# Induced attention followed by an ELU feed-forward: the opening and the ramp of the first batch in another written order

## The chip, the cores and the metric

One core of a Trainium2 chip runs the whole program. The metric is the device time of one execution in microseconds; the time before is the median of three runs. An execution has five engines with a list of instructions each: TensorE (PE, matmuls and transposes), VectorE (DVE), ScalarE (ACT), GpSimd (POOL) and SyncE (SP, which here only issues transfers). Each works its list in order and waits for the others by semaphores.

## What is computed

```python
scale = 1.0 / np.sqrt(C)                       # C = 128
def mab(q, kv):
    s = scale * (q @ kv.transpose(0, 2, 1))
    s = s - s.max(-1, keepdims=True)
    a = np.exp(s)
    a /= a.sum(-1, keepdims=True) + 1e-09
    return a @ kv
h = mab(I, x)                                  # I: 32 inducing points; x: 4 x 12480 x 128
y = mab(x, h).reshape(49920, 128)
f = y @ w_in                                   # w_in: 128 x 2048
g = np.where(f > 0.0, f, np.exp(np.minimum(f, 0.0)) - 1.0)
return g @ w_out                               # w_out: 2048 x 128
```

The weights come as float64, so the kernel sees each as pairs of 32-bit words.

## The kernel before, in words

A batch of 12480 rows is cut into 25 blocks of 480 or 512 rows, grouped in seven groups g = 0 to 6. The first attention of a batch gives h (32 x 128). It needs x transposed (xT), the scores of the inducing points, their running bounds in three phases for the first batch (`bias_of`), exponentials, and a gather of x with them. h times w_in gives the weight `hw` of 128 rows: three copies of 32 rows in high and low parts, and a row block of ones. The second attention of a block gives a stack `stk` (L576), and one matmul of `hw` with it is attention and first feed-forward layer at once (`ffn_in`, L613).

The long part is a loop over units. A unit is a block and a pair of chunks (256 of 2048 columns) of the feed-forward layer; a block has eight, planned as PPNPDPDP. For each, TensorE fills `ph`, ScalarE takes the exponential (e, L627), VectorE joins both branches (L633), then the result is split in a high part gh (ScalarE, L642) and a low part gl (GpSimd L655 for P, VectorE L649 for D, none for N), and TensorE adds up `po` from gh and gl with the second weight's high and low parts wo_h and wo_l, or from e with wo_n (`ffn_out`, L682). The output matmuls of unit n stand three to five units behind its input matmul in TensorE's list. `sum_excess` (L657) sums the second weight once, ahead of unit 7's output matmuls.

Only the first batch is not hidden. Its steps stand in `FIRST` (L35), a list of names that is worked from left to right; what a step issues is appended to its engines' lists in that order (TensorE, VectorE and ScalarE keep it; GpSimd and SyncE are put in order by the build in the unit loop). The names: x and y are the first and second half of a group's transposes with their copies to xT (`transpose_first`, L263, copies L290: VectorE for x, ScalarE for y), s and m the scores and their copy and maximum (L306), b the bound of a phase, w the exponentials (L378), e the transposed exponentials (L391), g and h the gather and its sum (L398). `sum`, `share`, `norm`, `spread`, `project`, `stack` make `hw` out of h, `room` allocates it and writes its ones (L483). l0 to l3 are the second attention of the first block alone (the lone block), a0 to a3 of the rest of group 0. u0, u1 and so on are the units: after a u the steps up to the next u are issued, in the loop of L856.

A to E, with a number s, turn part s of a weight into floating point: parts 0 to 3 are w_in, 4 to 7 are w_out, 512 columns each. A takes the exponent field out (VectorE L175, ScalarE L179), B makes a scale of it, bounded below and above (GpSimd L188 and L193; for some parts ScalarE L184 and L185 take the place of L188), C puts the mantissa together (VectorE L199, L203), D finishes (VectorE L209, product on GpSimd L213), E splits a part of w_out (ScalarE L236, L239, GpSimd L240) by chunks of 128. A part's exponent lies in one of two buffers of the pool `op`, so an A waits until the part two before it is done. The loads of the first batch stand in SyncE's list in the order of `first_batch` (L768): half of w_in, 14 pieces of x, the other half, four parts of w_out, which share buffers with later x.

Of the kernel before, what the change touches and what calls it, by code (L numbers as in the profile page):

```python
# [28 lines left out]


# [14 lines left out]
def kernel(  # L45
# [117 lines left out]
    class Weight:  # L163
# [17 lines left out]
        def scale_of(self, busy):  # L181
# [5 lines left out]
            else:  # L187
                nc.gpsimd.tensor_scalar(  # L188
                    out=self.scale, in0=self.part, scalar1=896.0, scalar2=1150.0,
                    op0=ALU.max, op1=ALU.min,  # L190
# [40 lines left out]
    def split_w_out(s, w):  # L231
        for i in range(WC):
            f = s * WC + i
            t = w.low[:, i * C : (i + 1) * C]
            if f in WHERE_N:
                nc.scalar.copy(wo_n[:, WHERE_N[f], :], t)  # L236
            if f in WHERE_S:
                n = WHERE_S[f]
                nc.scalar.copy(wo_h[:, n, :], t)  # L239
                nc.gpsimd.tensor_sub(wo_l[:, n, :], t, wo_h[:, n, :].bitcast(F32))  # L240
# [22 lines left out]
    def transpose_first(b, g):  # L263
# [9 lines left out]
        for v in range(0, U, UP):  # L273
# [13 lines left out]
            for i, half in enumerate(halves):  # L287
                m = min(2, nq - 2 * i)
                copy = nc.scalar.copy if v else nc.vector.tensor_copy
                copy(half[:, :, :, v : v + n], ps[:, 2 * i : 2 * i + m])  # L290
# [192 lines left out]
    def room_for_h(b):  # L483

        hw = hwp.tile([P, F], F32R, tag="hw", name=f"hw_{b}")
        nc.gpsimd.memset(hw[3 * Q :, :].bitcast(F32), 1.0)
# [430 lines left out]
```

## Time and profile before

| | us |
|---|---|
| median of three runs (1692.66 to 1695.55) | 1695.47 |
| the profiled execution | 1693.33 |
| its span in the trace | 1691.5 |
| TensorE busy | 1627.5 |
| ScalarE busy | 1478.7 |
| VectorE busy | 1428.5 |
| GpSimd busy | 1421.0 |

A row of the timeline reads: start and duration in us, engine, line of the kernel, operation, output and inputs with their shapes, and in brackets how long the engine was idle before it and what ended that. A row of the windows gives the busy time of TensorE, its weight loads, VectorE, ScalarE and GpSimd in a stretch, with the number of instructions, then the granted TensorE clock, the share of the DMA engines and GB/s. Rows that begin with a line number group all instructions of one kind: busy time and mean (page) or shortest, median and longest (view of a line).

### The profile page before, as it was taken

What the parts mean: (1) busy time and instruction counts of PE and PEld (TensorE: products, weight loads), DVE (VectorE), ACT (ScalarE), POOL (GpSimd) and SP (SyncE); (2) the same over time, 40 slices, a digit from 0 to 9 for tenths busy, and PEclk for the clock granted to TensorE, in tenths of its full rate; (3) what the DMA queues carried; (4) which work ended last, traced back from release to release, by engine and by line L of the source; (5) the groups of instructions that cost most, each with busy time, mean ns of one, the idle gap of its engine ahead of it and who ended that gap; (6) DMA issues with size and microseconds to landing.
All of it is one profiled execution on the core that took longest, in us unless ns stands there. A gap on an engine that the chain in (4) does not pass through costs nothing.

```text
span 1691.5 us, 23388 instructions
## 1 busy us (share of the span) xinstructions
PE 1627.5 (96%) x7656; PEld 1216.0 (72%) x7656; DVE 1428.5 (84%) x1479; ACT 1478.7 (87%) x1720; POOL 1421.0 (84%) x751
## 2 busy tenths in 40 slices
PE   6479999999999999999999999999999999999998
PEld 4246777777786777777877677777778777777886
DVE  6778888888889888888888888888888888888886
ACT  4368999999898999989989898899889999999996
POOL 4468888888898888888889898888888998998897
PEclk9689999999999999999999999999999999999999
DMA  7143324222314333232223423421322111110111
GB/s 252 40 83 67 62 49 82 53 50 73 75 38 79 52 75 69 45 73 58 57 66 55 78 48 63 82 50 22 79 44 44 28 25 35 34 37 16 33 28 24
DMA packets 384762, 98.18 MB, mean 58 GB/s; under 512 B 364864, under 2 KB 370784, under 8 KB 384384
## 3 DMA queue, kind: packets, MB, share of 16 engines
q1 hardware_dynamic: 384640, 96.68, 28.0%
q8 instruction: 61, 1.00, 0.3%
q14 instruction: 61, 0.50, 0.1%
HBM read 48.94 MB, written 25.56 MB: 44 GB/s over the span
## 4 chain that ended last, share of the span: by engine, by line
PE 72%; DVE 9%; ACT 7%; issue 6%; POOL 2%; DMA 2%; SPq 0%; POOLq 0%; DVEq 0%; ACTq 0%
PE po L704 51%; PE ph L619 17%; ACT e L627 4%; DVE e L633 3%; ACT gh L642 3%; POOL gl L655 1%; PE ps_t L532 1%; DVE xT L260 1%; DVE gl L649 1%; PE ps_s L313 1%; DVE ph L633 1%; PE ps_hh L404 1%; DMA xm<-in_x_dram 1%; DMA out_dram<-o 1%; DVE o L712 1%
## 5 line engine op out<-in xcount | busy, mean ns | idle before, releaser
L655 POOL TENSOR_TENSOR gl<-e,gh 128x1024 fp32r<-128x1024 f32 (+1 forms) x500 | 1169.5, 2355 | 213.2 <-ACT gh L642 201.6
L627 ACT ACTIVATE e<-ph 128x1024 f32<-128x1024 f32 (+1 forms) x800 | 800.8, 1002 | 122.8 <-PE ph L619 121.4
L633 DVE SCALAR_TENSOR_TENSOR e<-ph,e 128x1024 f32<-128x1024 f32 (+1 forms) x600 | 714.6, 1193 | 184.5 <-ACT e L627 178.6
L619 PE MATMUL ph<-stk,hw 128*128 128x512 f32 (+1 forms) x1600 | 541.3, 420 | 22.6 <-DVE e L633 15.9
L704 PE MATMUL po<-gh,wo_h 128*128 128x512 f32 (+1 forms) x1400 | 547.6, 391 | 11.1 <-ACT wo_h L239 6.8
L704 PE MATMUL po<-gh,wo_l 128*128 128x512 f32 (+1 forms) x1400 | 547.8, 391 | 2.6 <-POOL wo_l L240 2.6
L642 ACT ACTIVATE gh<-e 128x1024 fp32r<-128x1024 f32 (+1 forms) x500 | 518.6, 1037 | 27.5 <-DVE e L633 25.5
L704 PE MATMUL po<-gl,wo_h 128*128 128x512 f32 (+1 forms) x1400 | 433.0, 390 | 0.0
L619 PEld LDWEIGHTS ph<-stk,hw 128*128 128x128 f32 x1600 | 294.7, 190 | 170.8 <-issue 59.0
L704 PEld LDWEIGHTS po<-gh,wo_h 128*128 128x128 f32 x1400 | 263.6, 188 | 68.2 <-ACT wo_h L239 8.0
L704 PEld LDWEIGHTS po<-gl,wo_h 128*128 128x128 f32 x1400 | 264.2, 189 | 57.8
L704 PEld LDWEIGHTS po<-gh,wo_l 128*128 128x128 f32 x1400 | 263.8, 188 | 56.3 <-POOL wo_l L240 3.6
L633 DVE SCALAR_TENSOR_TENSOR ph<-ph,e 128x1024 f32<-128x1024 f32 (+1 forms) x200 | 239.5, 1198 | 30.2 <-ACT e L627 28.4
L649 DVE SCALAR_TENSOR_TENSOR gl<-ph,gh 128x1024 fp32r<-128x1024 f32 (+1 forms) x200 | 237.4, 1187 | 0.1
L642 ACT ACTIVATE gh<-ph 128x1024 fp32r<-128x1024 f32 (+1 forms) x200 | 201.1, 1005 | 4.3 <-DVE ph L633 3.9
L704 PE MATMUL po<-e,wo_n 128*128 128x512 f32 (+1 forms) x400 | 184.0, 582 | 0.0
L713 POOL TENSOR_TENSOR o<-o,excess 128x512 f32<-128x512 f32 (+1 forms) x100 | 126.6, 1266 | 4.4 <-DVE o L712 4.4
L704 PEld LDWEIGHTS po<-e,wo_n 128*128 128x128 f32 x400 | 75.4, 189 | 53.4 <-issue 46.0
L712 DVE STREAM_TRANSPOSE o<-po 128x512 f32<-128x512 f32 (+1 forms) x100 | 69.1, 691 | 4.9 <-PE po L704 4.9
L260 DVE STREAM_TRANSPOSE xT<-xq 128x1024 f32<-128x1024 f32 (+2 forms) x39 | 45.5, 1166 | 0.0
L592 POOL TENSOR_TENSOR alo<-aT,ahi 128x512 fp32r<-128x512 f32 (+3 forms) x27 | 34.2, 1269 | 0.8 <-ACT ahi L590 0.8
L404 PE MATMUL ps_hh<-xm,e 128*32 128x128 f32 (+2 forms) x872 | 31.1, 280 | 3.6 <-DVE h L421 2.0
(107 smaller groups left out, 552.6 us busy)
## 6 DMA issues: line engine op xcount, KB each, us to landing
xm<-in_x_dram SPq DMA_DIRECT2D x32, 512.0 KB, 4.8
out_dram<-o SPq DMA_DIRECT2D x240, 64.0 KB, 2.0
xq<-in_x_dram SPq DMA_DIRECT2D x84, 128.0 KB, 3.0
out_dram<-o SPq DMA_DIRECT2D x160, 60.0 KB, 1.9
stk<-ahi SPq DMA_DIRECT2D x118, 64.0 KB, 2.0
xq<-in_x_dram SPq DMA_DIRECT2D x60, 120.0 KB, 2.9
stk<-ahi SPq DMA_DIRECT2D x80, 60.0 KB, 2.0
stk<-alo SPq DMA_DIRECT2D x59, 64.0 KB, 2.0
```

The source lines that it names most:

```text
L260: nc.vector.transpose(t, xq.rearrange("p u d -> p (u d)"))
L404: nc.tensor.matmul(ps[c * Q : (c + 1) * Q, :C], st["e", g][:np_, u * Q : (u + 1) * Q], st["xm", g, u - u % UP][:np_, u % UP, :], start=(u ...
L592: eng.tensor_sub(alo, aT, ahi.bitcast(F32))
L619: nc.tensor.matmul(ph[:, i], state[b]["hw"][:, f * P : (f + 1) * P], stacks[b, k], start=True, stop=True,)
L627: nc.scalar.activation(e, ph, AF.Exp, bias=-1.0)
L633: nc.vector.scalar_tensor_tensor(out=v["g"], in0=v["ph"], scalar=1.0, in1=v["e"], op0=ALU.max, op1=ALU.min)
L642: nc.scalar.activation(v["gh"], v["g"], AF.Copy, bias=0.0 if how == "P" else -1.0)
L649: nc.vector.scalar_tensor_tensor(out=v["gl"], in0=v["g"], scalar=-1.0, in1=v["gh"].bitcast(F32), op0=ALU.add, op1=ALU.subtract,)
L655: nc.gpsimd.tensor_sub(v["gl"], v["e"], v["gh"].bitcast(F32))
L704: nc.tensor.matmul(po[:, :T], w, g, start=(cp == 0 and i == 0), stop=(cp == NCP - 1 and i == len(parts) - 1),)
L712: nc.vector.transpose(o.rearrange("p u d -> p (u d)"), po[:, :T])
L713: nc.gpsimd.tensor_tensor(out=o, in0=o, in1=excess.unsqueeze(1).broadcast_to([P, U, Q]), op=ALU.subtract)
```

## The change

The list `FIRST` is written anew. Group 1 opens instead of group 0, and all eight A stand ahead of the first unit, as do C, D of parts 4 and 5 and E of part 4. In detail:

- Of the 13 copies of transposed x that VectorE made, five stay (x of groups 1, 4 and 6), eight go to ScalarE (a table, `COPIES`).
- The first half of w_in is loaded behind four pieces of x, the second half ahead of the last piece (`LOADS`).
- ScalarE makes the bounds of parts 3 and 4 instead of 6 and 7.
- GpSimd's bounds are a min and then a max; they were a max and then a min.
- The ones of the first batch's `hw` come from ScalarE instead of GpSimd.
- E works on runs of neighbouring chunks, 512 or 256 columns, instead of 128. The split chunks are kept in their natural order, and `sum_excess` sums them in pieces of 256 columns.

```diff
-    x0 A0 A1 B0 x1 y0 C0 B1 D0 y1 s0 C1 m0 s1 x2 m1 y2 x3 s2 m2 y3 b0 w0 s3 x4 w1 m3 e0 y4
+    x1 x0 A1 y1 s1 A0 m1 B1 x2 y0 y2 x3 s0 C1 B0 s2 C0 m0 m2 D0 y3 x5 b0 w1 x4 w0 y4 x6 D1 A2 e1
...
+COPIES = "AA VA AA AA VA AA VA"
+LOADS = "0 1 2 3 i0 4 5 6 7 8 9 10 11 12 i1 13"
+BY_SCALAR = (3, 4)
...
-    CHUNKS_S = [f for how in "PD" for f in range(NFC) if PLAN[f // 2] == how]
+    CHUNKS_S = [f for f in range(NFC) if PLAN[f // 2] != "N"]
...
-                    out=self.scale, in0=self.part, scalar1=896.0, scalar2=1150.0,
-                    op0=ALU.max, op1=ALU.min,
+                    out=self.scale, in0=self.part, scalar1=1150.0, scalar2=896.0,
+                    op0=ALU.min, op1=ALU.max,
...
-                nc.scalar.copy(wo_h[:, n, :], t)
-                nc.gpsimd.tensor_sub(wo_l[:, n, :], t, wo_h[:, n, :].bitcast(F32))
+            for run in runs:
+                t = low[:, run[0] - part[0] : run[-1] + 1 - part[0], :]
+                to = slice(where[run[0]], where[run[-1]] + 1)
+                if whole:
+                    nc.scalar.copy(wo_n[:, to, :], t)
+                else:
+                    nc.scalar.copy(wo_h[:, to, :], t)
+                    nc.gpsimd.tensor_sub(wo_l[:, to, :], t, wo_h[:, to, :].bitcast(F32))
...
-                copy = nc.scalar.copy if v else nc.vector.tensor_copy
+                copy = nc.scalar.copy if COPIES.split()[g][v // UP] == "A" else nc.vector.tensor_copy
...
-        nc.gpsimd.memset(hw[3 * Q :, :].bitcast(F32), 1.0)
+        if steady:
+            nc.gpsimd.memset(hw[3 * Q :, :].bitcast(F32), 1.0)
+        else:
+            nc.scalar.activation(
+                hw[3 * Q :, :], largest[3 * Q :].broadcast_to([Q, F]), AF.Copy, scale=0.0, bias=1.0
+            )
...
-            steps[f"B{s}"] = lambda w=w, s=s: w.scale_of(s >= 6)
+            steps[f"B{s}"] = lambda w=w, s=s: w.scale_of(s in BY_SCALAR)
```

Behind the ramp, from unit 12 on, the order of every engine is row for row that of before. Three places ahead of it follow. Line numbers of the new kernel are larger by about 14 to 19.

The first is VectorE's list up to the bound of the first phase (`bias`), before and then now; `pm` are the maxima of a group's scores, `xT` the transposed x.

```order
L330 TENSOR_REDUCE pm_150<-s_0_272 128x1
L290 COPY xT_4_198<-ps_x_0_280 128x64x8
L290 COPY xT_5_199<-ps_x_0_280 128x64x8
L330 TENSOR_REDUCE pm_150<-s_1_291 128x1
L290 COPY xT_6_200<-ps_x_0_305 128x64x8
L290 COPY xT_7_201<-ps_x_0_305 128x32x8
L330 TENSOR_REDUCE pm_150<-s_2_321 128x1
L347 TENSOR_TENSOR apart_0_335<-pm_150,mine 128x4x3
L359 TENSOR_REDUCE bias_0_339<-ps_pm_0_337 128x1
```

```order
L344 TENSOR_REDUCE pm_150<-s_1_251 128x1
L204 SCALAR_TENSOR_TENSOR w_part<-w_raw,w_part 128x512
L208 TENSOR_SCALAR w_raw<-w_raw 128x512
L204 SCALAR_TENSOR_TENSOR w_part<-w_raw,w_part 128x512
L208 TENSOR_SCALAR w_raw<-w_raw 128x512
L344 TENSOR_REDUCE pm_150<-s_0_316 128x1
L344 TENSOR_REDUCE pm_150<-s_2_319 128x1
L214 SCALAR_TENSOR_TENSOR w_raw<-w_raw 128x512
L361 TENSOR_TENSOR apart_0_346<-pm_150,mine 128x4x3
L373 TENSOR_REDUCE bias_0_350<-ps_pm_0_348 128x1
```

The four copies have left this stretch; C of parts 1 and 0 and D of part 0 stand in it.

The second is VectorE's list from h transposed (`hT4`) to the lone block's transposed weights (`aT`), before and then now. w_raw_186 is part 4 of the weights, w_raw_188 part 5; the number behind `w_part` belongs to the same part.

```order
L460 COPY hT4_0_631<-ps_ht_0_629 128x128
L542 STREAM_TRANSPOSE s2_0_-1_635<-ps_t_0_-1_633 128x512
L175 TENSOR_SCALAR w_part_637<-w_raw_186 128x512
L480 TENSOR_TENSOR hw_l_0_646<-ps_hw_0_640,hw_h_0_645 128x512
L550 TENSOR_REDUCE mx2_0_-1_649<-s2_0_-1_635 128x16
L551 TENSOR_TENSOR s2_0_-1_635<-s2_0_-1_635,mx2_0_-1_649 128x512
L175 TENSOR_SCALAR w_part_653<-w_raw_188 128x512
L563 TENSOR_REDUCE sm2_0_-1_656<-s2_0_-1_635 128x16
```

```order
L474 COPY hT4_0_643<-ps_ht_0_641 128x128
L204 SCALAR_TENSOR_TENSOR w_part_614<-w_raw_188,w_part_614 128x512
L208 TENSOR_SCALAR w_raw_188<-w_raw_188 128x512
L561 STREAM_TRANSPOSE s2_0_-1_647<-ps_t_0_-1_645 128x512
L214 SCALAR_TENSOR_TENSOR w_raw_188<-w_raw_188 128x512
L569 TENSOR_REDUCE mx2_0_-1_649<-s2_0_-1_647 128x16
L570 TENSOR_TENSOR s2_0_-1_647<-s2_0_-1_647,mx2_0_-1_649 128x512
L204 SCALAR_TENSOR_TENSOR w_part_539<-w_raw_186,w_part_539 128x512
L208 TENSOR_SCALAR w_raw_186<-w_raw_186 128x512
L494 TENSOR_TENSOR hw_l_0_661<-ps_hw_0_655,hw_h_0_660 128x512
L582 TENSOR_REDUCE sm2_0_-1_664<-s2_0_-1_647 128x16
```

The two A (L175) are gone from here, and C and D of part 5 and C of part 4 have come; D of part 4 follows a few rows later. As built, C and D of part 5 stand ahead of those of part 4, although `FIRST` names them behind u0: the A of part 6, ahead of u0, needs that part's buffer.

The third is GpSimd's list from the preparation of parts 4 and 5 to the first low part gl, before and then now; w_part_699 and w_part_702 are the exponents of parts 7 and 6.

```order
L188 TENSOR_SCALAR w_part_637<-w_part_637 128x512
L193 TENSOR_SCALAR w_part_637<-w_part_637 128x512
L188 TENSOR_SCALAR w_part_653<-w_part_653 128x512
L193 TENSOR_SCALAR w_part_653<-w_part_653 128x512
L655 TENSOR_TENSOR gl_0_738<-e_0_693,gh_0_709 128x1024
L213 TENSOR_TENSOR w_raw_186<-w_raw_186,w_part_637 128x512
L240 TENSOR_TENSOR wo_l_128<-w_raw_186,wo_h_127 128x128 x4
```

```order
L218 TENSOR_TENSOR win_sb_125<-w_raw_182,w_part_418 128x512
L501 MEMSET hw_1_4001 32x2048
L193 TENSOR_SCALAR w_part_614<-w_part_614 128x512
L198 TENSOR_SCALAR w_part_614<-w_part_614 128x512
L678 MEMSET ones_923 128x128
L218 TENSOR_TENSOR w_raw_188<-w_raw_188,w_part_614 128x512
L218 TENSOR_TENSOR w_raw_186<-w_raw_186,w_part_539 128x512
L254 TENSOR_TENSOR wo_l_128<-w_raw_186,wo_h_127 128x512
L193 TENSOR_SCALAR w_part_699<-w_part_699 128x512
L193 TENSOR_SCALAR w_part_702<-w_part_702 128x512
L198 TENSOR_SCALAR w_part_699<-w_part_699 128x512
L673 TENSOR_TENSOR gl_0_742<-e_0_711,gh_0_727 128x1024
```

The products and the first split of w_out now stand ahead of the first gl, and between them and it the bounds of parts 7 and 6, which ScalarE made before.

More of the change, by code (lines that the diff above doesn't have):

```diff
@@ L150 @@
     win_sb = const.tile([C, F], F32, name="win_sb")
-    wo_n = const.tile([P, len(CHUNKS_N), C], F32, name="wo_n")
+    if CHUNKS_N:
+        wo_n = const.tile([P, len(CHUNKS_N), C], F32, name="wo_n")
     wo_h = const.tile([P, NSPLIT, C], F32R, name="wo_h")
@@ L231, in split_w_out @@
     def split_w_out(s, w):
[L232 to L240, printed above, removed]
+        low = w.low.rearrange("p (c d) -> p c d", d=C)
+        part = range(s * WC, (s + 1) * WC)
+        for where, whole in ((WHERE_N, True), (WHERE_S, False)):
+            mine = [f for f in part if f in where]
+            runs = []
+            for f in mine:
+                if runs and runs[-1][-1] == f - 1:
+                    runs[-1].append(f)
+                else:
+                    runs.append([f])
+            for run in runs:
[6 more added lines that the diff above has]
+                    nc.gpsimd.tensor_sub(wo_l[:, to, :], t, wo_h[:, to, :].bitcast(F32))
     xT = {}
@@ L638, in ffn_split @@
         v, how = live[n], plan(n)
-        shape = list(v["e"].shape)
         if how != "N":
-            v["gh"] = ghp.tile(shape, F32R, tag="gh", name=f"gh_{n}")
-            nc.scalar.activation(v["gh"], v["g"], AF.Copy, bias=0.0 if how == "P" else -1.0)
+            v["gh"] = ghp.tile(list(v["e"].shape), F32R, tag="gh", name=f"gh_{n}")
+            nc.scalar.activation(v["gh"], v["g"], AF.Copy, bias=-1.0 if how == "D" else 0.0)
     def ffn_low(n):
         v, how = live[n], plan(n)
-        shape = list(v["e"].shape)
+        if how == "N":
+            return
+        v["gl"] = glp.tile(list(v["e"].shape), F32R, tag="gl", name=f"gl_{n}")
+        gh = v["gh"].bitcast(F32)
         if how == "D":
-            v["gl"] = glp.tile(shape, F32R, tag="gl", name=f"gl_{n}")
             nc.vector.scalar_tensor_tensor(
-                out=v["gl"], in0=v["g"], scalar=-1.0, in1=v["gh"].bitcast(F32),
-                op0=ALU.add, op1=ALU.subtract,
-            )
-        if how == "P":
-            v["gl"] = glp.tile(shape, F32R, tag="gl", name=f"gl_{n}")
-            nc.gpsimd.tensor_sub(v["gl"], v["e"], v["gh"].bitcast(F32))
+                out=v["gl"], in0=v["g"], scalar=-1.0, in1=gh, op0=ALU.add, op1=ALU.subtract
+            )
+        else:
+            nc.gpsimd.tensor_sub(v["gl"], v["e"], gh)
     def sum_excess():
@@ L660, in sum_excess @@
         nc.gpsimd.memset(ones, 1.0)
-        n_p = sum(PLAN[f // 2] == "P" for f in CHUNKS_S)
-        n_n = len(CHUNKS_N)
-        parts = [
-            (ones_r, w[:, i : min(i + 4, n_p), :]) for w in (wo_h, wo_l) for i in range(0, n_p, 4)
-        ]
-        parts += [(ones, wo_n[:, i : min(i + 4, n_n), :]) for i in range(0, n_n, 4)]
-        ps = bank("ps_excess")
+        parts = []
+        for cp in range(NCP):
+            f = 2 * cp
+            if PLAN[cp] == "P":
+                i = WHERE_S[f]
+                parts += [(ones_r, wo_h[:, i : i + 2, :]), (ones_r, wo_l[:, i : i + 2, :])]
+            if PLAN[cp] == "N":
+                parts.append((ones, wo_n[:, WHERE_N[f] : WHERE_N[f] + 2, :]))
+        ps = bank("ps_excess")[:, : 2 * C]
         for i, (one, w) in enumerate(parts):
-            m = w.shape[1] * C
             nc.tensor.matmul(
-                ps[:, :m], one, w.rearrange("p c d -> p (c d)"),
+                ps, one, w.rearrange("p c d -> p (c d)"),
                 start=i == 0, stop=i == len(parts) - 1,
```

20 lines of the change are left out of this document (12 added, 8 removed).

## The prediction

> **What bounds the kernel now.** I read the page's busy times first, then the windows of three stretches, to see whether one engine sets the pace everywhere.
>
> ```profile
> PE 1627.5 (96%) x7656; PEld 1216.0 (72%) x7656; DVE 1428.5 (84%) x1479; ACT 1478.7 (87%) x1720; POOL 1421.0 (84%) x751
> ...
> core 0: us, PE busy (x) PEld busy (x) DVE busy (x) ACT busy (x) POOL busy (x), PEclk, DMA share, GB/s
> 400.00:800.00 400.00, 396.48 (x1874) 295.08 (x1873) 344.97 (x352) 362.63 (x417) 345.14 (x175) 1.00 0.31 61
> ...
> 10.00:60.00 50.00, 35.56 (x396) 23.32 (x395) 37.33 (x73) 19.67 (x42) 23.56 (x20) 0.89 0.50 164
> 60.00:118.00 58.00, 32.88 (x91) 21.04 (x91) 46.17 (x51) 31.61 (x49) 35.34 (x31) 0.72 0.37 74
> ```
>
> In the steady part TensorE is busy 396.5 of 400 us at full clock. There an instruction of another engine costs nothing, and whatever makes TensorE saturate earlier moves the end by the same amount. From 60 to 118 us it is busy 32.9 of 58, at a clock of 0.72. So the question is when saturation begins. I take as mark the output matmuls of unit 8, the last to start behind a marked wait in the ramp. The timeline of TensorE shows how it gets there.
>
> ```profile
> 63.35 2.93 PE L619 MATMUL ph<-stk,hw 128*128 128x512 f32 x6 [6.70 <-DVE stk L585]
> 72.51 0.79 PE L704 MATMUL po<-gh,wo_h 128*128 128x512 f32 x1 [4.35 <-ACT wo_h L239]
> ...
> 81.30 1.22 PE L619 MATMUL ph<-stk,hw 128*128 128x512 f32 x2 [4.98 <-DVE e L633]
> ...
> 108.17 0.79 PE L704 MATMUL po<-gh,wo_l 128*128 128x512 f32 x1 [2.62 <-POOL wo_l L240]
> ...
> 117.95 0.50 PE L704 MATMUL po<-gh,wo_h 128*128 128x512 f32 x1 [0.79 <-DVE s L542]
> ```
>
> First unit at 63.35, unit 8's output at 117.95. The waits name the first part of the second weight (wo_h), VectorE's list, and the last part (wo_l). Everything the change touches lies before 117.95; behind it every engine's list is the same. The sum is therefore how much earlier than 117.95 unit 8 comes.
>
> **The opening, up to h.** Three rows of VectorE mark it: the third score bound and the normalised h; the pair of copies shows the price of what leaves.
>
> ```profile
> 27.10 1.29 DVE L290 COPY xT<-ps_x 128x512 f32<-128x512 f32 x2 [1.84 <-PE ps_x L281]
> ...
> 42.47 0.19 DVE L359 TENSOR_REDUCE bias<-ps_pm 128x1 f32<-128x28 f32 x1 [0.50 <-PE ps_pm L356]
> ...
> 45.11 1.23 DVE L432 SCALAR_TENSOR_TENSOR es<-es,scale,es 128x1 f32<-128x1 f32 x1
> ...
> 46.44 0.22 DVE L432 SCALAR_TENSOR_TENSOR es<-es,scale,es 128x1 f32<-128x1 f32 x1
> ...
> 49.82 0.97 DVE L451 TENSOR_SCALAR hn<-h,r 128x128 f32<-128x128 f32 x1
> ...
> L290 DVE COPY xT<-ps_x x13: 410/679/692, 10.1 to 35.3; 128x512 f32<-128x512 f32 x12, 128x256 f32<-128x256 f32 x1
> L290 ACT COPY xT<-ps_x x13: 378/586/592, 14.3 to 35.7; 128x512 f32<-128x512 f32 x7, 128x448 f32<-128x448 f32 x5, 128x256 f32<-128x256 f32 x1
> ```
>
> VectorE is busy 37.3 of the 50 us from 10 to 60, ScalarE 19.7, so VectorE's list sets the opening. 8 of its 13 copies go to ScalarE: 8 x 0.645 (1.29 a pair) = 5.2 us off the list ahead of the bound. On ScalarE they cost 8 x 0.586 = 4.7 us, inside its free 30; the scores now queue behind them there, which I price at nothing because the bound of the first phase waits for its third group in either order. The Trainium skill, ScalarE: Activation LUTs, section "Rules for kernel authors", tells one to put simple elementwise work on VectorE rather than ScalarE. By it the copies would be dearer where they go; the two rows say 0.586 against 0.679 us, so the row decides, and by the rule taken at face value the opening would gain nothing.
>
> The sum of es at 45.11 takes 1.23 us where its twin takes 0.22, beside a GpSimd multiply; that multiply (third part of the first weight) comes earlier now, so 1.0 us goes. h is normalised 5.2 + 1.0 = 6.2 us earlier, at 43.6. The two ends: 0, if ScalarE's queue holds the scores as long as VectorE did, and 7.5, if min before max is as fast as the add and multiply (below).
>
> The loads: the first tile transposed is now the third piece of x.
>
> ```profile
> 8.05 1.97 PE L281 MATMUL ps_x<-ident,xm 128*128 128x128 f32 x8 [5.16 <-DMA xm<-in_x_dram]
> 10.58 4.72 PE L281 MATMUL ps_x<-ident,xm 128*128 128x128 f32 x24 [0.56 <-DMA xm<-in_x_dram]
> ```
>
> At 8.05 1.5 MB had come (1 MB of weight, one piece of x of 0.5 MB), at 10.58 2.5 MB. Three pieces are 1.5 MB too, so the first transpose stays at 8.05. The half of the first weight, now behind four pieces, is complete at 3 MB, near 11.8 at that rate; the products that need it come after the first scores. I take 0, and 0.5 either way.
>
> **From h to the first unit.** C and D of the second weight's first two parts move here, ahead of the lone block's steps; A of both moves out.
>
> ```profile
> 47.35 0.67 DVE L199 SCALAR_TENSOR_TENSOR w_part<-w_raw,w_part 128x512 uint32<-128x512 uint32 x1
> 48.05 0.43 DVE L203 TENSOR_SCALAR w_raw<-w_raw 128x512 uint32<-128x512 uint32 x1
> ...
> 48.65 0.69 DVE L209 SCALAR_TENSOR_TENSOR w_raw<-w_raw 128x512 f32<-128x512 uint32 x1
> ...
> 56.57 0.69 DVE L480 TENSOR_TENSOR hw_l<-ps_hw,hw_h 128x512 fp32r<-128x512 f32 x1 [1.35 <-ACT hw_h L478]
> ...
> 55.95 0.59 ACT L478 CAST hw_h<-ps_hw 128x512 fp32r<-128x512 f32 x1 [11.02 <-PE ps_hw L468]
> ...
> 50.76 1.80 POOL L486 MEMSET hw<- 32x2048 f32 x1
> ...
> L627 ACT ACTIVATE e<-ph 128x1024 f32<-128x1024 f32 (+1 forms) x800 | 800.8, 1002 | 122.8 <-PE ph L619 121.4
> ...
> 59.00 1.92 POOL L188 TENSOR_SCALAR w_part<-w_part 128x512 f32<-128x512 uint32 x1 [1.07 <-DVE w_part L175]
> 61.00 0.66 POOL L193 TENSOR_SCALAR w_part<-w_part 128x512 uint32<-128x512 f32 x1
> ```
>
> One C and D is 0.67 + 0.43 + 0.69 = 1.8 us; two are 3.6. C5 also waits for GpSimd: behind the last product of the first weight stand a memset for the next batch (1.80), the bounds (1.92) and add-multiply (0.66), and the transposes of the lone block queue behind C5 on VectorE; I put 0.7 us for that. Against these 4.3 us stand the 1.35 us wait for hw_h, which C4 now fills, and the two A that leave, one-input operations like the 0.43 above: net 2.1 later. If nothing is filled it is 4.3, if other waits are filled too, 0. First unit: 63.35 - 6.2 + 2.1 = 59.25, 4.1 earlier.
>
> The row of ones leaves GpSimd (one of two 1.80 memsets). On ScalarE nothing shows 32 x 2048; from 0.59 at 512 and 1.00 at 1024 I estimate 1.9 us, hidden in the 11.02 us that ScalarE waits for ps_hw; bare it would cost 1.9. Bounds as min, max: the trace has no such pair; 0.66 and 1.92 are the nearest ends, I take 1.92, the same two operations. The scalar pair for parts 3 and 4 instead of 6 and 7 is the same work, elsewhere.
>
> **The ramp.** VectorE's list is the thread, as its waits are short and its busy time 46 of 58 us. These are the rows that are longer than their kind, the wait for the excess, and the tail of the last weight.
>
> ```profile
> 60.49 0.69 DVE L571 TENSOR_TENSOR s_-1_635<-s_-1_635,sm_-1_656 128x512 f32<-128x512 f32 x1
> ...
> 69.30 1.60 DVE L569 TENSOR_SCALAR sm<-sm 96x16 f32<-96x16 f32 x1
> 71.22 1.45 DVE L571 TENSOR_TENSOR s<-s,sm 96x512 f32<-96x512 f32 x1
> 77.22 2.89 DVE L592 TENSOR_TENSOR alo<-aT,ahi 96x512 fp32r<-96x512 f32 x1 [0.73 <-ACT ahi L590]
> 86.18 2.58 DVE L209 SCALAR_TENSOR_TENSOR w_raw<-w_raw 128x512 f32<-128x512 uint32 x1
> 97.46 2.48 DVE L203 TENSOR_SCALAR w_raw<-w_raw 128x512 uint32<-128x512 uint32 x1
> 114.10 1.19 DVE L676 TENSOR_REDUCE excess<-ps_excess 32x32 f32<-32x128 f32 x4 [6.30 <-PE ps_excess L670]
> ...
> 77.21 2.35 POOL L655 TENSOR_TENSOR gl<-e,gh 128x1024 fp32r<-128x1024 f32 x1
> ...
> 99.97 0.69 DVE L209 SCALAR_TENSOR_TENSOR w_raw<-w_raw 128x512 f32<-128x512 uint32 x1
> ...
> 107.66 1.73 POOL L240 TENSOR_TENSOR wo_l<-w_raw,wo_h 128x128 fp32r<-128x128 f32 x4
> ...
> L633 DVE SCALAR_TENSOR_TENSOR e<-ph,e 128x1024 f32<-128x1024 f32 (+1 forms) x600 | 714.6, 1193 | 184.5 <-ACT e L627 178.6
> ```
>
> From the first unit to the excess are 114.10 - 63.35 = 50.75 us. What goes: (1) C and D of two parts, 3.6. (2) The wait of 6.30 for the excess, if the last part is split in time. (3) The two caught operations at 69.30 and 71.22, 1.4 + 0.8 = 2.2: their partner was the first GpSimd difference (gl), and where they stand now GpSimd does the bounds of parts 7 and 6, beside which the same multiply took its plain 0.69 at 60.49 (the bounds at 59.00 quoted above). The other three caught ones (2.2 + 1.9 + 2.0) I leave: their kind still stands beside gl. That makes 50.75 - 12.1 = 38.65, the excess at 59.25 + 38.65 = 97.9, unit 8 another 3.85 later (117.95 - 114.10): 101.75, against 117.95 a gain of 16.2 us.
>
> Does the last part come in time? Its D was at 99.97, 36.6 after the first unit. Two passes of ELU, a difference and a transpose stand behind it now instead of ahead (4 x 1.2 = 4.8), and 3.6 + 2.2 are gone: 26 after, so 85.3. Its wo_l ended 9.4 us behind D (109.39), over two gl; now one of 2.4 less lies between: 7, so 92.3. The matmuls from there to the excess took 5.9 (108.17 to 114.10): 98.2. Both ways agree within half a microsecond.
>
> The wide pieces: four subtractions took 1.73; one of 512 columns is not in the trace, the 1024 columns of gl give about 1.2. ScalarE's four copies become one of 0.59 (its 512-wide cast). Under 1 us a part and off the thread, 0 taken. The Trainium skill, GPSIMD Engine Reference, section "Key points", says that GpSimd and VectorE share their SBUF interfaces, and that a VectorE instruction with two SBUF inputs contends. The row at 77.22, as long as the gl at 77.21, agrees. By it a wide subtraction holds VectorE 1.2 us where a piece held it 0.4: 4 x 0.8 = 3.2 us lost at most, 13.0 instead of 16.2. The sum of the excess takes eleven matmuls of 256 columns for seven of up to 512, the same columns: 0. SyncE's loads of the second x tile of the next batch wait for part 5's wo_l and now stand ahead of the transfers of the stacks of blocks 1 to 3; the first to need those is unit 8's input, far behind, so 0, and if part 5 came last of all, it would be the wait for it that I count under the first rival.
>
> **The rivals.** *The ramp keeps its length.* The last part still ends late, behind gl and the bounds, and the 6.30 us wait stays: gain 16.2 - 6.3 = 9.9, at worst the 4.1 of the first unit; 1685 to 1691. For it: GpSimd has the same work in the ramp and now two bounds in a row ahead of gl. Chance 0.16.
>
> *More than forecast.* The remaining caught operations (6.1 us) go as well, and TensorE, with shorter gaps, keeps its clock: one matmul took 0.79 at 108.17 and 0.50 at 117.95, so the 5.9 us ahead of the excess could be 3.7. Gain 22 to 26 (with the 2.1 of the part above filled): 1669 to 1673. The Trainium skill, TensorE: Matmul & The Clock Gate, section "Why this matters for your kernels", warns of idle gaps over about 3 us; the gaps of 4.35 and 4.98 with a mean clock of 0.72 agree. Chance 0.13.
>
> *Slower.* The pair min, max is slow on GpSimd. It stands in front of C2, C5 and, twice, the first gl: four on the path. It decides at 16.2 / 4 = 4.1 us more each, that is 6.0 us an operation against 1.92; at 7 the kernel takes 1679.3 + 4 x 5.1 = 1699.7. No row comes near. Chance 0.04.
>
> *Nothing comes through.* What is won in the ramp is paid back, since ScalarE (363 of 400 us) and VectorE cannot keep ahead of a TensorE that starts early: 1693 to 1697. Against it: the steady row has TensorE, not ScalarE, without gaps. Chance 0.05.
>
> **How the numbers follow.** The forecast has 0.62. The profiled execution took 1693.33 (span 1691.5 and 1.8 around it), 2.1 below the median of three, 1695.47, which is what will be compared: 1695.5 - 16.2 = 1679.3. Bounds: all ends good 25 us (1670), the wait kept and the wide pieces paid 16.2 - 6.3 - 3.2 = 6.7 (1689). Left out are most of the last two rivals and the edges. Faster by over 0.2% (3.4 us, about what a measurement of this kernel can tell) holds the first three cases but for a tail: 0.91; within 0.05; slower 0.04.
>
> **What would show it.** Right: the third bound near 37, hn near 43.6, the first unit's matmul near 59, the wait before the excess under 1 us, unit 8's output near 101, the steady windows unchanged. Wrong: the multiply by sm still over 1.4 us, the bounds far from 1.92, ScalarE's score copies late, or a new wait on wo_l behind 100.

## The result, and the profile after

The changed kernel takes 1677.15 us (median of four runs, 1676.45 to 1679.47) against 1695.49 for the kernel before beside it (1692.66 to 1695.55): ratio 0.9898, 95% interval 0.9881 to 0.9915. The forecast was 1679.3. The profiled execution took 1677.49, its span is 1675.7.

The total is as forecast, and its split is not. The marks of the prediction, in us of the profiled executions:

| | before | forecast | after |
|---|---|---|---|
| first transpose | 8.05 | 8.05 | 9.21 |
| third score bound | 42.47 | about 37 | 43.62 |
| hn | 49.82 | 43.6 | 52.77 |
| first unit | 63.35 | 59.25 | 66.07 |
| first unit to excess | 50.75 | 38.65 | 32.14 |
| first unit to unit 8's output (the ramp) | 54.60 | 42.5 | 35.82 |
| unit 8's output | 117.95 | 101.75 | 101.89 |

The opening lost 2.7 us where 4.1 were to be won, and the ramp won 18.8 where 12.1 were forecast: two errors of nearly 7 us that cancel. First the page's busy times and the windows of the new kernel (columns as in the windows of before).

```profile
PE 1624.8 (97%) x7660; PEld 1214.5 (72%) x7660; DVE 1412.2 (84%) x1471; ACT 1483.1 (89%) x1718; POOL 1408.5 (84%) x740
...
10.00:60.00 50.00, 38.92 (x401) 25.12 (x399) 31.06 (x66) 27.53 (x56) 15.14 (x19) 0.80 0.56 164
60.00:118.00 58.00, 44.09 (x163) 30.07 (x164) 50.98 (x64) 43.40 (x52) 42.62 (x25) 0.85 0.48 94
400.00:800.00 400.00, 396.49 (x1875) 295.31 (x1874) 344.92 (x352) 361.99 (x416) 343.81 (x174) 1.00 0.32 62
```

The steady stretch is the same to 0.01 us. From 60 to 118 us TensorE is busy 44.1 of 58 us instead of 32.9, at a clock of 0.85 instead of 0.72; this stretch now reaches 16 us past the ramp's end. From 10 to 60 VectorE has 6.3 us less to do, and yet the opening did not end earlier. TensorE's timeline:

```profile
9.21 4.38 PE L295 MATMUL ps_x<-ident,xm 128*128 128x128 f32 x24 [6.32 <-DMA xm<-in_x_dram]
...
32.42 2.37 PE L295 MATMUL ps_x<-ident,xm 64*128 64x64 f32 x14 [2.33 <-DMA xm<-in_x_dram]
...
66.07 2.93 PE L638 MATMUL ph<-stk,hw 128*128 128x512 f32 x6 [6.07 <-DVE stk L604]
...
84.49 1.22 PE L638 MATMUL ph<-stk,hw 128*128 128x512 f32 x2 [3.55 <-DVE e L652]
...
94.65 0.50 PE L723 MATMUL po<-gh,wo_l 128*128 128x512 f32 x1 [0.35 <-POOL wo_l L254]
...
101.89 0.47 PE L723 MATMUL po<-gh,wo_h 128*128 128x512 f32 x1 [0.66 <-DVE s L561]
```

The transposes at 32.42 are those of the last half group (y6): TensorE stands 2.33 us for the last piece of x, and the first gather and the phase's bound are queued behind them. The 2.62 us wait for wo_l is down to 0.35. VectorE shows both sides:

```profile
36.91 0.18 DVE L373 TENSOR_REDUCE bias<-ps_pm 128x1 f32<-128x20 f32 x1 [2.54 <-PE ps_pm L370]
...
43.62 0.19 DVE L373 TENSOR_REDUCE bias<-ps_pm 128x1 f32<-128x28 f32 x1 [0.65 <-PE ps_pm L370]
...
45.61 0.22 DVE L446 SCALAR_TENSOR_TENSOR es<-es,scale,es 128x1 f32<-128x1 f32 x1
...
49.98 2.11 DVE L180 TENSOR_SCALAR w_part<-w_raw 128x512 uint32<-128x512 uint32 x1 [1.41 <-POOL win_sb L218]
...
52.77 0.29 DVE L465 TENSOR_SCALAR hn<-h,r 128x128 f32<-128x128 f32 x1
...
70.63 0.17 DVE L588 TENSOR_SCALAR sm<-sm 96x16 f32<-96x16 f32 x1
...
71.12 0.69 DVE L590 TENSOR_TENSOR s<-s,sm 96x512 f32<-96x512 f32 x1
...
74.91 0.73 DVE L208 TENSOR_SCALAR w_raw<-w_raw 128x512 uint32<-128x512 uint32 x1
...
80.82 0.69 DVE L611 TENSOR_TENSOR alo<-aT,ahi 96x512 fp32r<-96x512 f32 x1 [1.43 <-ACT ahi L609]
...
82.61 0.69 DVE L214 SCALAR_TENSOR_TENSOR w_raw<-w_raw 128x512 f32<-128x512 uint32 x1
...
98.21 0.92 DVE L695 TENSOR_REDUCE excess<-ps_excess 32x32 f32<-32x64 f32 x4 [0.26 <-PE ps_excess L689]
```

Two new waits stand in the opening: the second bound comes 2.5 us late behind TensorE, and A of part 5 (49.98), right ahead of the last sums of h, waits 1.41 us for its buffer and then takes 2.11 us instead of 0.43. In the ramp all five caught operations (held by a GpSimd operation beside them) are back near their plain price (0.17, 0.69, 0.73, 0.69, 0.69), not two, and the wait for the excess is 0.26 instead of 6.30. A third wait stands ahead of the first bound, and it is for ScalarE. One row of VectorE before, then ScalarE and VectorE of the changed kernel; s (L337, before L323) are the scores that ScalarE copies:

```profile
23.64 0.69 DVE L330 TENSOR_REDUCE pm<-s 128x1 f32<-128x512 f32 x1 [0.37 <-ACT s L323]
```

```profile
17.52 3.80 ACT L304 COPY xT<-ps_x 128x512 f32<-128x512 f32 x8 [0.43 <-PE ps_x L295]
21.13 1.27 ACT L337 COPY s<-ps_s 128x512 f32<-128x512 f32 x2
...
17.20 0.69 DVE L344 TENSOR_REDUCE pm<-s 128x1 f32<-128x512 f32 x1 [3.45 <-ACT s L337]
...
21.84 1.28 DVE L344 TENSOR_REDUCE pm<-s 128x1 f32<-128x512 f32 x2 [1.83 <-ACT s L337]
```

VectorE's maxima wait 5.3 us for score copies, where it was 0.4 before. Eight copies of transposed x stand right ahead of two of the score copies on ScalarE. GpSimd shows what A5 ran beside, the bounds, and the last split:

```profile
50.01 1.80 POOL L501 MEMSET hw<- 32x2048 f32 x1
52.26 0.61 POOL L193 TENSOR_SCALAR w_part<-w_part 128x512 f32<-128x512 uint32 x1 [0.45 <-DVE w_part L180]
...
68.62 1.42 POOL L193 TENSOR_SCALAR w_part<-w_part 128x512 f32<-128x512 uint32 x2 [1.17 <-DVE w_part L180]
...
88.37 1.30 POOL L254 TENSOR_TENSOR wo_l<-w_raw,wo_h 128x512 fp32r<-128x512 f32 x1
...
93.27 1.33 POOL L254 TENSOR_TENSOR wo_l<-w_raw,wo_h 128x512 fp32r<-128x512 f32 x1
```

A5 ends with the memset. A bound by min, max takes 0.61 us, not 1.92. Three things were left to find out: what holds the opening, what each edit is worth in the ramp, and whether the opening's loss can be taken back.

### The profile page after: what moved, and what is told of

Its sections match the earlier page's. It is cut to its first block, busy times and chain, and to the rows that moved or that the text cites. A ratio compares the mean times of both kernels' runs of the same rounds, so it can differ in the third digit from the quotient of the medians.

```text
span 1675.7 us, 23394 instructions
## 1 busy us (share of the span) xinstructions
PE 1624.8 (97%) x7660; PEld 1214.5 (72%) x7660; DVE 1412.2 (84%) x1471; ACT 1483.1 (89%) x1718; POOL 1408.5 (84%) x740
## 4 chain that ended last, share of the span: by engine, by line
PE 73%; DVE 9%; ACT 8%; issue 6%; DMA 2%; POOL 2%; SPq 0%; POOLq 0%; DVEq 0%; ACTq 0%
PE po L723 51%; PE ph L638 18%; ACT e L646 4%; ACT gh L660 3%; DVE e L652 3%; DMA xm<-in_x_dram 2%; PE ps_t L551 1%; DVE gl L669 1%; DVE xT L274 1%; PE ps_hh L418 1%; DVE ph L652 1%; POOL gl L673 1%; PE ps_s L327 1%; DMA out_dram<-o 1%; DVE o L731 0%
## 5 line engine op out<-in xcount | busy, mean ns | idle before, releaser
L731 DVE STREAM_TRANSPOSE o<-po 128x512 f32<-128x512 f32 (+1 forms) x100 | 69.1, 691 | 4.9 <-PE po L723 4.9
```

Source lines behind the costliest of these rows:

```text
L731: nc.vector.transpose(o.rearrange("p u d -> p (u d)"), po[:, :T])
```

## The experiments

All marks in us of each profiled execution; the last column is the median of its runs. From unit 8's output to the end of the span all of them take 1573.3 to 1573.9 us (before: 1573.55), so the mark of unit 8 gives the time of its own execution within 0.6 us. How far executions of one kernel lie apart is seen in the runs' ranges.

| kernel | third bound | hn | first unit | ramp | unit 8's output | median |
|---|---|---|---|---|---|---|
| before | 42.47 | 49.82 | 63.35 | 54.60 | 117.95 | 1693.6 to 1695.5 |
| changed | 43.62 | 52.77 | 66.07 | 35.82 | 101.89 | 1677.15 |
| changed, again | 42.88 | 51.84 | 65.15 | 35.81 | 100.96 | 1676.40 |
| loads as before | 39.86 | 49.03 | 62.33 | 36.73 | 99.06 | 1673.85 |
| copies as before | 41.95 | 51.12 | 63.37 | 36.70 | 100.07 | 1675.25 |
| late loads' steps later | 40.63 | 49.71 | 63.00 | 35.81 | 98.81 | 1674.89 |
| A5 later | 41.24 | 48.67 | 62.37 | 35.80 | 98.17 | 1675.19 |
| max, min | 42.37 | 51.55 | 64.54 | 38.09 | 102.63 | 1678.08 |
| narrow pieces | 42.55 | 51.72 | 65.02 | 35.84 | 100.86 | 1675.53 |
| before with min, max | 40.53 | 47.88 | 61.51 | 54.51 | 116.02 | 1691.00 |
| before with the list alone | 44.02 | 51.52 | 66.74 | 37.37 | 104.11 | 1679.82 |
| old opening, new ramp | 41.72 | 51.24 | 65.99 | 35.79 | 101.78 | 1676.95 |
| both moves | 40.93 | 48.38 | 62.03 | 36.46 | 98.49 | 1673.94 |
| loads as before, A5 later | 40.42 | 47.87 | 61.72 | 37.14 | 98.86 | 1673.07 |

**The changed kernel again.** No edit; the base.

> The changed kernel once more, unaltered, as the base of this set of runs. What is profiled of the opening differs between three profiles of the same list by up to 2.4 us at the third bound (41.24, 42.37, 43.62), the landing of the loads being the only thing in it that is not fixed by the program. If that is chance of a single execution: third bound anywhere from 41 to 44, from hn on as before (hn to unit 8's output 49.1), time 1675.5 to 1678.

Measured 1676.40 (1676.17 to 1676.92), 0.9900 of before (0.9882 to 0.9917). Five profiles have this list up to the third bound (one of them with dearer bounds on GpSimd), and it lies at 41.24 to 43.62; hn to unit 8's output is 49.12 in both profiles of the changed kernel. Two things make these 2.4 us. The transposes of the last half group start at 31.30 to 32.42, as the last piece lands. And behind TensorE's wait for that piece its clock falls to 0.50 for 3.4 us in four of the five profiles, while the kernel with A5 later keeps 1.00 there. The transposes and the gather behind them, first in the base, then in that kernel:

```profile
31.86 2.48 PE L295 MATMUL ps_x<-ident,xm 64*128 64x64 f32 x14 [2.24 <-DMA xm<-in_x_dram]
34.27 1.70 PE L418 MATMUL ps_hh<-xm,e 128*32 128x128 f32 x32
```

```profile
31.76 1.56 PE L295 MATMUL ps_x<-ident,xm 64*128 64x64 f32 x14 [2.26 <-DMA xm<-in_x_dram]
33.25 1.08 PE L418 MATMUL ps_hh<-xm,e 128*32 128x128 f32 x32
```

The same work takes 4.0 to 4.2 us in the four and 2.6 in the fifth. So the landing moves the opening by 1.1 us from one execution to the next, and the clock by 1.3 to 1.6.

**The loads in the order of before.**

```diff
-LOADS = "0 1 2 3 i0 4 5 6 7 8 9 10 11 12 i1 13"
+LOADS = "i0 0 1 2 3 4 5 6 7 8 9 10 11 12 13 i1"
```

> The changed kernel with the loads in the order of before (first half of the weight ahead of x, second half behind it). Forecast's view: the order of loads is worth 0, either way 0.5: third bound 43 to 44. Rival: a piece of x takes the queue longer per byte than the weight, so x first only moved the first transpose from 8.05 to 9.2, and the half ahead of the last piece held up the last group: first transpose near 8 to 10, but the last pieces land 1 to 2 us earlier, second bound 34 to 35, time 1675 to 1676. Second rival: A1 and A0 now stand behind three transposes, so with the weight first, x comes later and the time goes up 1 to 3 us.

Measured 1673.85 (1673.19 to 1675.22), 2.5 us less than the base, with a first transpose at 10.53, 1.5 later. The first rival holds for the end of the loads, and for more than it said, though the first transpose is not at 8 to 10; the forecast and the second rival fall. The DMA view of the first 45 us gives size and median time from issue to landing; first the changed kernel, then this one:

```profile
q1 hardware_dynamic: 4272, 10.60, 77.7%
...
w_raw<-in_moe_w_in_dram SPq DMA_DIRECT2D x2, 1024.0 KB, 12.3
```

```profile
q1 hardware_dynamic: 4272, 10.60, 69.1%
...
w_raw<-in_moe_w_in_dram SPq DMA_DIRECT2D x2, 1024.0 KB, 8.2
```

The same 4272 packets and 10.60 MB keep the engines busy 77.7% of the stretch in the new order and 69.1% in the old: in the new order a transfer takes longer. Why it does stays open. The second bound's wait is 0.55 instead of 2.54, and the clock doesn't fall there:

```profile
33.32 0.18 DVE L373 TENSOR_REDUCE bias<-ps_pm 128x1 f32<-128x20 f32 x1 [0.55 <-PE ps_pm L370]
```

**The copies as before.**

```diff
-COPIES = "AA VA AA AA VA AA VA"
+COPIES = "VA VA VA VA VA VA VA"
```

> The changed kernel with the copies of transposed x as before (x halves on VectorE, y halves on ScalarE). Forecast's view: 8 copies of 0.645 us are on VectorE's path, the third bound comes 5.2 us later than in the changed kernel and the time rises to about 1682. Rival (the opening is bound by the landing of the loads and by TensorE's queue, VectorE waits anyway): third bound within 1 us, time within 1 us of the changed kernel.

Measured 1675.25 (1675.01 to 1676.17). The third bound lies among the five of the base, the time 1.1 us below it. With these loads the eight copies that left VectorE are worth nothing; the rival holds, its 1 us in time nearly. Only the first bound knew them (26.14 against 24.56 in the base); the second waits for the last loads in the base, and here it comes at 35.39 with a wait of 0.55, while TensorE no longer stands for the last piece. With the loads of before no run undoes the copies.

**The steps that wait for the last loads, later.**

```diff
...
-D1 A2 e1 e0 s3 s4 m3 m4 y6 A3 w2 B2 y5 g0 b1 h0 w3 C2 e2
+D1 e1 e0 s3 s4 m3 m4 w2 y5 g0 b1 h0 y6 A2 A3 B2 w3 e2 C2
...
```

> The changed kernel, with the steps that wait for the last loads (A of parts 2 and 3, transposes and copies of the last half group, B2) moved behind the scores and maxima of groups 3 and 4, the bound of the second phase and what follows it. Theory L (queues behind late loads cost the opening 3 to 4 us): second bound 33 to 35 instead of 36.91, hn 49 to 51 instead of 52.77, time 1673 to 1676. Rival O (VectorE's and ScalarE's lists are full there anyway, the wait only moves): hn within 1 us of 52.77, time within 1.5 us of 1677.

Measured 1674.89 (1674.31 to 1675.29). The second bound is at 32.17 with a wait of 0.55, 2.5 to 4.7 us earlier than in the five of the base; at the third bound 0.6 to 3.0 of that is left, at unit 8 2.2 against the base. Theory L holds in place; in size it is 2.1 us at hn and 1.5 in time against the base, not 3 to 4.

**A5 later.**

```diff
...
-D3 A5 h5 g6 B5 h6 norm room spread l0
+D3 h5 g6 h6 norm room spread A5 B5 l0
...
```

> The changed kernel, with A and B of part 5 put behind spread instead of ahead of the last sums of h. Theory W: the 1.41 us wait and the 2.11 us of A5 on VectorE, right ahead of the last sums, cost the path of h about 3.5 us: hn 49 to 50 instead of 52.77, first unit near 63 to 64, time near 1674. Rival G (given back: C5, D5 come later by as much, and with them wo_h and the ramp): hn earlier too, but unit 8's output within 1 us of 101.89 and the time within 1 us of 1677.

Measured 1675.19 (1673.75 to 1676.87). Third bound to hn is 7.43 us, in the base 8.96 and in the changed kernel's first profile 9.15: 1.5 to 1.7, not 3.5. VectorE now waits for the gather instead (here the last two sums):

```profile
46.48 0.35 DVE L430 SCALAR_TENSOR_TENSOR h<-h,scale,ps_hh 128x128 f32<-128x128 f32 x1 [0.42 <-PE ps_hh L418]
48.34 0.29 DVE L435 TENSOR_TENSOR h<-h,ps_hh 128x128 f32<-128x128 f32 x1 [1.51 <-PE ps_hh L418]
```

So half of A5's 3.5 us lay beside TensorE's gather. Of what is won, 0.4 is paid in hn itself, which now runs beside the memset and takes 0.72 instead of 0.29. W holds in kind; G does not, as the ramp keeps its 35.80. The rest of this kernel's early unit 8 (98.17) is not the edit's: its second bound, ahead of the edit, was already at 34.70, as its clock didn't fall there. Its runs reach into the base's.

**The bounds as max, min, in the changed kernel.**

```diff
-                    out=self.scale, in0=self.part, scalar1=1150.0, scalar2=896.0,
-                    op0=ALU.min, op1=ALU.max,
+                    out=self.scale, in0=self.part, scalar1=896.0, scalar2=1150.0,
+                    op0=ALU.max, op1=ALU.min,
```

> The changed kernel, with GpSimd's bounds as a max and then a min again (all five of them 1.92 us instead of 0.61). Theory A (they lie beside other work in the ramp; only the first gl waits for two of them, and its wait is followed by idle time on the path's engines): 1677 to 1680 us, first unit within 0.5 us of 66.07. Theory B (the cheap pair carries part of the 18 us, because several bounds stand right ahead of products or of C on the path): 1682 us or more, excess later than 101.

Measured 1678.08 (1677.74 to 1679.10), 1.7 over the base; the ramp is 2.28 longer. The time is as A said. Its first unit (64.54) is not within 0.5 us of 66.07, mostly since its last piece of x landed earliest of the five. First GpSimd, then VectorE of this kernel:

```profile
67.09 4.02 POOL L193 TENSOR_SCALAR w_part<-w_part 128x512 f32<-128x512 uint32 x2 [1.17 <-DVE w_part L180]
...
71.77 2.36 POOL L673 TENSOR_TENSOR gl<-e,gh 128x1024 fp32r<-128x1024 f32 x1
```

```profile
72.53 2.14 DVE L204 SCALAR_TENSOR_TENSOR w_part<-w_raw,w_part 128x512 uint32<-128x512 uint32 x1
```

The two bounds take 4.02 instead of 1.42, so the first gl starts 7.23 us behind the first unit instead of 5.87, and C of part 7 (0.68 where nothing is beside it) is caught for nearly all of it. From there on VectorE's rows lie 1.36 us later than in the base, counted from the first unit: that is the bounds' share, at the place that A named. The other 0.92 comes only at the excess, and there the clocks differ: in this execution it is 0.50 from 25.5 to 28.9 us behind the first unit, in the base 1.00. The two kernels above with ramps of 36.7, whose bounds are cheap, are longer at the excess by the same 0.9, and their clock is at 0.50 from 23.8 to 27.4. So 0.92 of the 2.28 is put down to the clock.

**The kernel before with its bounds as min, max.** The same two lines the other way round.

> The kernel before, with nothing but GpSimd's bounds as a min and then a max. Both theories expect 0.6 us an operation there. Theory A: off the path, time of before less 0 to 1.5 us (1694 to 1695.5). Theory B: about 5 us faster than before (1690).

Measured 1691.00 (1690.29 to 1691.68), ratio 0.9984 (0.9975 to 0.9993): 2.6 us, between both theories. All that the profile shows is won ahead of hn: 0.6 at the first bound (25.08 to 24.45), 1.9 at the third and at hn; the ramp stays at 54.51. In the old list the bounds stood on the opening's path, not on the ramp's.

**The second weight in narrow pieces.**

```diff
...
-                    nc.scalar.copy(wo_h[:, to, :], t)
-                    nc.gpsimd.tensor_sub(wo_l[:, to, :], t, wo_h[:, to, :].bitcast(F32))
...
+                nc.scalar.copy(wo_h[:, n, :], t)
+                nc.gpsimd.tensor_sub(wo_l[:, n, :], t, wo_h[:, n, :].bitcast(F32))
```

> The changed kernel with the second weight split in chunks of 128 columns again. Forecast's view: the width is worth 0 (under 1 us a part, off the thread): time within 1 us of 1676.4, ramp (first unit to unit 8's output) 35.8 as now. Rival N (four small subtractions let VectorE go between them, a wide one holds it): 2 to 3 us faster. Rival W (four copies and four subtractions, 1.73 against 1.30 us a part on GpSimd and 1.6 against 0.65 on ScalarE, stand in the ramp's chain): ramp 37 to 39.

Measured 1675.53 (1674.52 to 1676.46), ramp 35.84: worth nothing, as forecast. The last wo_l ends 29.5 us behind the first unit instead of 28.5, which nobody waits for.

**The new list alone.**

```diff
-    x0 A0 A1 B0 x1 y0 C0 B1 D0 y1 s0 C1 m0 s1 x2 m1 y2 x3 s2 m2 y3 b0 w0 s3 x4 w1 m3 e0 y4
+    x1 x0 A1 y1 s1 A0 m1 B1 x2 y0 y2 x3 s0 C1 B0 s2 C0 m0 m2 D0 y3 x5 b0 w1 x4 w0 y4 x6 D1 A2 e1
...
-            steps[f"B{s}"] = lambda w=w, s=s: w.scale_of(s >= 6)
+            steps[f"B{s}"] = lambda w=w, s=s: w.scale_of(s in (3, 4))
```

> The kernel before with the new list alone (and ScalarE's bounds for parts 3 and 4, which the list needs); loads, copies, max then min, ones on GpSimd and the narrow pieces stay as before. Theory R (the order of the ramp is the change, the rest is small): the ramp, first unit to unit 8's output, falls from 54.6 to 38 to 40 (35.8 and the 2.3 of the dear bounds, and up to 2 for the narrow pieces), time 1676 to 1680. Rival H (list and edits only work together): ramp over 44, time over 1684.

Measured 1679.82 (1678.13 to 1680.13), ramp 37.37. Theory R holds: the order brings 17.2 of the ramp's 18.8 us, and 13.8 of 16 to 17 at unit 8. Its ramp is even shorter than R had it. Of the 1.6 us that are left in the ramp, 1.3 stand at C of part 7 already, caught there as in the kernel with max, min.

**The old opening with the new ramp.** Loads, copies and list as before up to `spread`, then:

```diff
+spread A4 B4 A5 B5 l0 l1 C4 project l2 D4 stack l3 a0 E4 a1 A7 A6 u0
```

> The old opening with the new ramp: the changed kernel, but loads, copies and the list up to spread as before, with A and B of parts 4 and 5 right behind spread; from l0 on the new list. Theory R (all the gain is in the ramp; the new opening gains nothing): third bound 40 to 41 and hn 47.5 to 48.5, as in the kernel before with cheap bounds (40.53, 47.88), first unit 61.5 to 62.5, ramp near 36, unit 8's output 97.5 to 98.5, time 1672.5 to 1674. Forecast's view (the new opening is worth 5 us and more by its copies): hn 5 us later than the new opening gives with the old loads (49.03), time over 1678.

Measured 1676.95 (1676.81 to 1678.00). The ramp is 35.79, as R said; the opening is not: hn comes at 51.24, 3.4 us later than in the kernel before with min, max. Two steps that ScalarE makes in the changed kernel now stand on its path. One is the row of ones, between two score copies; VectorE waits 1.85 us behind it. The other is B3, ahead of the exponentials of the third phase (43.51), which start 1.8 us behind the bound instead of 0.4. ScalarE, and in the second row VectorE:

```profile
37.62 1.90 ACT L503 ACTIVATE hw<-largest 32x2048 fp32r<-32x2048 f32 x1
...
40.14 0.64 DVE L344 TENSOR_REDUCE pm<-s 64x1 f32<-64x480 f32 x1 [1.85 <-ACT s L337]
...
42.14 0.70 ACT L189 ACTIVATE w_part<-w_part,rebias 128x512 f32<-128x512 uint32 x1
...
43.51 0.68 ACT L396 ACTIVATE s<-s,bias 128x480 f32<-128x480 f32 x1
```

So this is not the old opening alone, and what that is worth with the new ramp stays open. As it stands here it is no better than the new one, and no worse by time, which the forecast had 6 us faster.

**Both moves**, A5 and the late loads' steps.

> The changed kernel with both moves: A and B of part 5 behind spread, and the steps that wait for the last loads behind those that don't. If the two gains are apart (1.75 us from third bound to hn; 1 to 3 us up to the third bound): third bound near 40.6, hn near 48.0, unit 8's output near 97.4, time about 1673. If they are one and the same idle time of VectorE: no better than the better of the two alone (1674.9).

**The loads as before, and A5 later.**

> The changed kernel with the loads in the order of before and A, B of part 5 behind spread. If the two gains add up: third bound 39.9 as with the loads alone, 7.4 from there to hn instead of 9.2, hn 47.3, unit 8's output near 97.3, time 1672 to 1673. If A5's wait only covered idle time of the gather on TensorE: hn near 48.5 and time near 1674.

Measured 1673.94 (1673.62 to 1674.23) and 1673.07 (1672.32 to 1674.01). Both take 7.45 from the third bound to hn, as with A5 later alone (7.43), and reach hn (48.38 and 47.87) 0.4 and 0.6 us behind the sum of the gains. But unit 8 comes 1.1 and 1.6 us later than that sum, as both ramps are longer, 36.46 and 37.14, through the same list with the same waits up to 23.5 us behind the first unit. The windows of equal places in the ramp, 18 to 23 and 23.5 to 28.5 us behind the first unit, tell why; first the changed kernel, then the last one (the column behind the five engines is the clock):

```profile
84.07:89.07 5.00, 3.93 (x10) 2.86 (x10) 5.00 (x6) 4.15 (x5) 4.01 (x3) 0.66 0.33 82
89.60:94.60 5.00, 4.69 (x19) 3.49 (x19) 3.57 (x4) 4.67 (x6) 5.00 (x5) 1.00 0.99 203
```

```profile
79.72:84.72 5.00, 4.59 (x10) 3.15 (x10) 5.00 (x6) 3.60 (x4) 4.00 (x3) 0.50 0.33 80
85.25:90.25 5.00, 4.99 (x13) 3.98 (x14) 3.44 (x3) 4.37 (x6) 4.66 (x4) 0.57 0.95 197
```

TensorE issues 19 matmuls in five us at full clock and 13 at 0.57. In both the clock falls around the same gap (3.55 and 3.63 us). Windows of one us place its fall and rise, in the changed kernel and in this one:

```profile
83.50:84.50 1.00, 0.01 (x1) 0.01 (x1) 1.00 (x2) 0.03 (x1) 1.00 (x1) 0.79 0.34 84
...
86.50:87.50 1.00, 1.00 (x4) 0.81 (x3) 1.00 (x2) 0.69 (x2) 1.00 (x1) 0.50 0.44 107
87.50:88.50 1.00, 0.92 (x4) 0.42 (x3) 1.00 (x2) 0.87 (x1) 1.00 (x2) 1.00 0.27 66
```

```profile
78.50:79.50 1.00, 0.00 (x0) 0.00 (x0) 1.00 (x2) 0.00 (x0) 0.48 (x1) 0.93 0.43 110
...
89.50:90.50 1.00, 1.00 (x5) 0.81 (x5) 0.07 (x1) 0.58 (x1) 1.00 (x1) 0.95 0.47 184
```

A mean of 0.79 between 1.00 and 0.50 puts the fall at 84.08, and the rise is at 87.5: 3.4 us. Here it is 79.36 to 89.6, 10.2 us, so the matmuls ahead of the excess run at half clock and 1.3 us of ramp is lost. With both moves the dip is 6.8 us (81.62 to 88.44) and the ramp in between. The ramps of the ten profiles with the new ramp and cheap bounds go by it: 35.8 in the six where the clock is back at 1.00 by 22.7 us behind the first unit, 36.5 to 37.1 in the four where it is 0.50 until 26.4 to 27.9. What sets the length of the dip was steered by no kernel here and stays open. By its median the last kernel is the fastest: its four runs (1672.32 to 1674.01) lie below all eight of the changed kernel (1676.17 to 1679.47), its ratio to before is 0.9874 (0.9858 to 0.9890); they overlap with those of both moves and of the loads alone.

## Why the prediction was right, and where it was wrong

**That the end follows unit 8's output one to one: right.** From that mark to the end all profiles take the same within 0.6 us.

**"8 x 0.645 ... = 5.2 us off the list": the step that failed.** The durations were right (0.589 us a copy on ScalarE, median of 21), and VectorE is busy 6.3 us less. But the opening wasn't VectorE's any more. Ahead of the first bound it waits 5.3 us for ScalarE's score copies, the term that I "price at nothing"; it is the lower end that I named, and my sign "ScalarE's score copies late". Undoing the copies costs 1.6 us at the first bound. The second bound waits for the last piece of x with these loads, and there undoing them costs nothing. The row that argued for it, VectorE busy 37 of 50 us, is an average over the opening; it does not say which wait ends last at a bound. How much of the 5.2 us would come with other loads stays open: with the loads as before VectorE still waits 6.0 us for score copies, and with A5 later as well hn comes at 47.87, not 43.6. The rule of the Trainium skill (ScalarE: Activation LUTs, "Rules for kernel authors") would have had no gain either, but not for this reason: the copy itself is still the cheaper one on ScalarE.

**The loads, "I take 0, and 0.5 either way": failed.** They cost 2.5 us. I priced the bytes ahead of the first transpose, at the rate seen in the old order; the price sat at the last piece, and the rate itself fell. Of the 3.0 us at the third bound, 1.3 to 1.6 are the half clock behind the wait for that piece (an estimate from the five profiles of the base).

**The blocked sum of es, 1.0 us: right** (0.22 at 45.61), and lost in the rest.

**From h to the first unit, "net 2.1 later": mis-sized.** 13.53 became 13.30, near the bound "0" at which other waits are filled too. In this hn itself became 0.68 shorter (0.97 to 0.29, as no GpSimd product runs beside it now), so behind its end 0.45 was added. What was missed is A5 ahead of h: an A that waits for a buffer, with a memset beside it, 1.5 to 1.7 us up to hn. I had looked at the A that leave the lone block, not at the queue that they were moved into.

**The row of ones:** 1.905 us on ScalarE (estimate 1.9), and nobody waited for it in the changed kernel; in the old opening VectorE waited 1.85 us behind it. **Wide pieces, 0:** right. The Trainium skill's rule on two SBUF inputs (GPSIMD Engine Reference, "Key points") agrees with C of part 7 in the kernel with max, min, held 2.14 us beside gl; beside the wide pieces stand only VectorE operations with at most one SBUF input, and these take their usual time (the ELU pass, with one input from PSUM, 1.19 at 88.37 beside the wide piece of the same start in the changed kernel).

**The bounds, "I take 1.92": wrong end.** 0.61; worth 1.4 us in this ramp without the clock, and 1.7 in time.

**The ramp: right in kind, 6.7 us short.** The wait for the excess went (6.0), C and D of two parts (3.6) and the first two caught operations (2.2) went. "The other three caught ones I leave" failed: they went too, 2.2 + 1.9 + 2.0 = 6.1 us, since the operations now stand between GpSimd's two-input operations (alo starts at 80.82, 0.1 us ahead of the end of the third gl, and GpSimd is free from there to 83.38); 0.5 us is left, at C of part 7 (0.88 and 0.73 for 0.68 and 0.43). That was my rival "more than forecast", which I gave 0.13; its second half, the warm clock, came with it (eleven matmuls of the excess from 96.39 to 98.0). The rival "slower", by min, max, turned out to be a gain.

So the number is right by luck: what was over-counted in the opening (6.8 us) and under-counted in the ramp (6.7) happen to be of one size. Only the ramp's mechanism was confirmed.

## What to carry to other kernels

Before taking work off an engine, look at which wait ends last at each mark along the stretch, not at the engine's share of it: an opening that is fed by loads can be bound by the last piece, as this one was, and a step that needs that piece belongs behind everything that doesn't, on every in-order engine. An operation that waits for a buffer is priced by what is queued behind it. And a gain ahead of a ramp can be shortened by the clock, so compare marks, not only times; and before a difference of marks is put down to an edit, compare the clock in the stretch ahead of them, which moved marks by 0.7 to 1.6 us here.
